# Ordering the transfers of a fused attention and FFN kernel by need, with part of its vector work and transposes moved to GpSimd and DMA

## Chip, cores, metric

One core of one Trainium2 chip. The metric is the device time of one execution in microseconds (us), lower is better.

## The reference, cut to what matters

Performer attention (random features, no softmax matrix) over 8 batches of 8 heads, 576 positions and head dimension 64, then a two-layer FFN with quick GELU over the 4608 tokens.

```python
def phi(x):                                   # x is q or k, scaled
    h = x @ omega.T - sum(x*x)/2              # 128 features
    return np.exp(h - h.max(-1)) / np.sqrt(m)
kv  = k_p^T @ v;  z = k_p.sum(positions)      # per head
num = q_p @ kv;   den = q_p @ z + 1e-6
x   = (num / den) as 4608 x 512
out = quick_gelu(x @ w_in) @ w_out            # 512 -> 2048 -> 512
```

## The kernel before

An attention **round** `p` handles two heads of one batch, four rounds to a batch. `item_pk` and `item_pq` project k and q and take the exponential, `vp` is v divided by the row maximum of k's features, `item_kv` and `item_nd` are the two products with it, and `item_xt` transposes the result `xb` into `xt`, the FFN's input. Other tiles named below: `kT` and `qT` are the transposed k and q, `sk` and `sq` their casts in DRAM, `kvs` is the copy of the `kv` product, `xps` TensorE's transpose of `xb` before it is copied, `gT` the FFN's hidden layer after the GELU, `win` and `wout` the FFN's weights, `osb` the output. The FFN works on nine **blocks** of 512 tokens; between its groups of four matmuls the rounds of a later batch are strewn. Only TensorE's order is fixed by hand; on the other engines a scheduler orders the instructions.

```python
def load_cast(b, n, h0, h1):      # f32 DRAM -> bf16 DRAM scratch, issued by GpSimd
    nc.gpsimd.dma_start(tiles[b]["s" + n][...], rows[...])
def load_tr(b, n, h0, h1):        # scratch -> transposed SBUF tile, issued by SyncE
    nc.sync.dma_start_transpose(tiles[b][n][...], tiles[b]["s" + n][...])
# ... cut: load_v, load_win, load_wout ...

def item_pk(p, i):
    pk = ps_pp.tile(...)          # six matmuls on 64 rows, 128 columns each
    nc.scalar.activation(out=ke, in_=pk, func=AF.Exp, scale=SCALE)
    nc.vector.reduce_max(out=maxE[:], in_=ke6, axis=AX.X)
    nc.vector.reciprocal(out=emax[:], in_=maxE[:])
    nc.vector.tensor_tensor(out=vp[:, :, 0:64], in0=v, in1=emax, op=ALU.mult)   # forms cut
    nc.vector.tensor_copy(out=vp[:, :, 64], in_=emax[:])

def item_xt(p):
    for t, c0 in enumerate(CHUNKS):
        nc.tensor.transpose(xps[:, c0 : c0 + 128], xb[:, t, :], ident[:])
    nc.vector.tensor_copy(out=xt[c][:, b * S : (b + 1) * S], in_=xps[:])

# a round: pk 0, kv, pk 1, nd 0, pq 0, nd 1, pq 1, xt  (the old round's items between the new one's)
ctx.enter_context(tc.manual_schedule(engines={mybir.EngineType.PE}))
# casts of batch 0, its v and transposes, all of win, batch 1, all of wout; then
for i in range(NBLK + 1):
    if i + 2 < B:
        load_batch(i + 2)
    # FFN groups of block i and i - 1, with the items of four rounds between them
```

The softmax here doesn't subtract the row's maximum and nothing guards it: scores larger than these inputs give would overflow.

Of the kernel before, what the change touches and what calls it, by code (L numbers as in the profile page):

```python
# [20 lines left out]
def kernel(  # L21
# [10 lines left out]
    nc = tc.nc  # L32
# [75 lines left out]
    def load_cast(b, n, h0, h1):  # L108
        rows = qrows if n == "q" else krows
        r0 = b * H * S2  # L110
        nc.gpsimd.dma_start(
            tiles[b]["s" + n][h0 * S2 : h1 * S2, :], rows[r0 + h0 * S2 : r0 + h1 * S2, :]
        )
# [20 lines left out]

    st = {}

    def item_pk(p, i):
        b, h = p // NPAIR, (p % NPAIR) * 2 + i
        kT = tiles[b]["k"]
        pk = ps_pp.tile([128, 2, 512], F32, name="pk", tag="pp")  # L140
        for c in range(3):
            for par in range(2):
                lo = par * 64
                nc.tensor.matmul(  # L144
                    pk[0:KP, par, c * 128 : (c + 1) * 128],
                    lhsT=kT[lo : lo + 64, h * S2 + c : (h + 1) * S2 : 3],
                    rhs=omT2[lo : lo + 64, :],
                )
        ke = work.tile([KP, 2, 384], BF16, name="ke", tag="ke")
        nc.scalar.activation(out=ke[:], in_=pk[0:KP, :, 0:384], func=AF.Exp, scale=SCALE)  # L150
        ke6 = ke[:].rearrange("p two (c f) -> p (two c) f", c=3)
        maxE = small.tile([KP, 6], F32, name="maxE", tag="maxE")
        nc.vector.reduce_max(out=maxE[:], in_=ke6, axis=AX.X)  # L153
        vp = work.tile([KP, 6, 65], BF16, name="vp", tag="vp")
        emax = small.tile([KP, 6], F32, name="emax", tag="emax")
        nc.vector.reciprocal(out=emax[:], in_=maxE[:])
        nc.vector.tensor_tensor(  # L157
            out=vp[:, :, 0:64].rearrange("p (two c) d -> p two c d", two=2),
            in0=tiles[b]["v"][:, h, :].rearrange("p (c two d) -> p two c d", c=3, two=2),
            in1=emax[:].rearrange("p (two c) -> p two c", two=2).unsqueeze(3).to_broadcast([KP, 2, 3, 64]),  # L160
            op=ALU.mult,
        )
        nc.vector.tensor_copy(out=vp[:, :, 64], in_=emax[:])
        st[p, "ke", i] = ke
        st[p, "vp", i] = vp

    def item_pq(p, i):
        b, h = p // NPAIR, (p % NPAIR) * 2 + i
        qT = tiles[b]["q"]
        pq = ps_pp.tile([128, 2, 512], F32, name="pq", tag="pp")  # L170
        for par in range(2):
            lo = par * 64
            nc.tensor.matmul(  # L173
                pq[:, par, 0:S2],
                lhsT=omT2[lo : lo + 64, :],
                rhs=qT[lo : lo + 64, h * S2 : (h + 1) * S2],
            )
        qe = work.tile([128, S], BF16, name="qe", tag="qe")
        nc.scalar.activation(  # L179
            out=qe[:].rearrange("p (two r) -> p two r", two=2),  # L180
            in_=pq[:, :, 0:S2],
            func=AF.Exp,
            scale=SCALE,
        )
        st[p, "qe", i] = qe

    def item_kv(p):
        kv = ps_m.tile([128, 2, 65], F32, name="kv", tag="m")
        for i in range(2):
            ke, vp = st.pop((p, "ke", i)), st.pop((p, "vp", i))  # L190
            for t in range(6):
                nc.tensor.matmul(  # L192
                    kv[:, i, :],
                    lhsT=ke[:, t // 3, (t % 3) * 128 : (t % 3 + 1) * 128],
                    rhs=vp[:, t, :],
                    start=(t == 0),
                    stop=(t == 5),
                )
        kvs = work.tile([128, 2, 65], BF16, name="kvs", tag="kvs")
        nc.scalar.activation(out=kvs[:], in_=kv[:], func=AF.Copy)  # L200
        st[p, "kvs"] = kvs

    def item_nd(p, i):
        if i == 0:
            st[p, "xb"] = work.tile([128, NCH, 128], BF16, name="xb", tag="xb")
        xb, kvs, qe = st[p, "xb"], st[p, "kvs"], st.pop((p, "qe", i))
        nd = ps_m.tile([128, NCH, 65], F32, name="nd", tag="m")
        for t, c0 in enumerate(CHUNKS):
            nc.tensor.matmul(nd[:, t, :], lhsT=qe[:, c0 : c0 + 128], rhs=kvs[:, i, :])  # L209
        rden = small.tile([128, NCH], F32, name="rden", tag="rden")  # L210
        nc.vector.reciprocal(out=rden[:], in_=nd[:, :, 64])  # L211
        nc.vector.tensor_tensor(  # L212
            out=xb[:, :, i * 64 : (i + 1) * 64],
            in0=nd[:, :, 0:64],
            in1=rden[:].unsqueeze(2).to_broadcast([128, NCH, 64]),
            op=ALU.mult,
        )

    def item_xt(p):
        b, c = p // NPAIR, p % NPAIR  # L220
        xb = st.pop((p, "xb"))
        st.pop((p, "kvs"))
        xps = ps_m.tile([128, S], BF16, name="xps", tag="m")
        for t, c0 in enumerate(CHUNKS):
            nc.tensor.transpose(xps[:, c0 : c0 + 128], xb[:, t, :], ident[:])  # L225
        nc.vector.tensor_copy(out=xt[c][:, b * S : (b + 1) * S], in_=xps[:])  # L226

    NP = B * NPAIR

    def round_items(p):  # L230
        its = []
        if p < NP:
            its.append(lambda: item_pk(p, 0))
        if p >= 1:
            its.append(lambda: item_kv(p - 1))
        if p < NP:
            its.append(lambda: item_pk(p, 1))
        if p >= 1:
            its.append(lambda: item_nd(p - 1, 0))
        if p < NP:  # L240
            its.append(lambda: item_pq(p, 0))
        if p >= 1:
            its.append(lambda: item_nd(p - 1, 1))
        if p < NP:
            its.append(lambda: item_pq(p, 1))
        if p >= 1:
            its.append(lambda: item_xt(p - 1))
        return its


    gTs = {}
# [22 lines left out]
    def mm2(i, r, part, pool, tag):  # L274
        if part == 0:
            pos[0] = pool.tile([128, DM], F32, name="po", tag=tag)
        po = pos[0]
        gT = gTs[i]
        for f in range(part * 4, part * 4 + 4):
            nc.tensor.matmul(  # L280
                po[:],
                lhsT=gT[:, f, r * 128 : (r + 1) * 128],
                rhs=wout[:, f, :],
                start=(f == 0),
                stop=(f == NFC - 1),
            )
        if part == 3:
            osb = osbp.tile([128, DM], F32, name="osb", tag="osb")
            nc.scalar.activation(out=osb[:], in_=po[:], func=AF.Copy, scale=0.5)  # L289
            c0 = i * TB + r * 128  # L290
            end = c0 + 128
            p0 = 0
            while c0 < end:
                run = c0 // S2
                n = min(end, (run + 1) * S2) - c0
                row = (run // 2) * S + 2 * (c0 - run * S2) + run % 2
                nc.sync.dma_start(
                    out[row : row + 2 * n - 1 : 2, :], osb[p0 : p0 + n, :]
                )
                c0 += n  # L300
                p0 += n


    ctx.enter_context(tc.manual_schedule(engines={mybir.EngineType.PE}))

    load_begin(0)
    for n in ("k", "q"):
        load_cast(0, n, 0, 2)
    for n in ("k", "q"):
        load_cast(0, n, 2, H)  # L310
    load_v(0, 0, 2)
    for n in ("k", "q"):
        load_tr(0, n, 0, 2)
    load_v(0, 2, H)
    for n in ("k", "q"):
        load_tr(0, n, 2, H)
    for j in range(4):
        load_win(j)
    load_batch(1)
    for j in range(4):  # L320
        load_wout(j)

    for p in range(NPAIR + 1):
        for it in round_items(p):
            it()

    for i in range(NBLK + 1):
        if 2 <= i + 2 < B + 0 and i + 2 < B:
            load_batch(i + 2)
        items = []  # L330
        for p in range((i + 1) * NPAIR + 1, (i + 2) * NPAIR + 1):
            if p <= NP:
                items += round_items(p)
        quanta = []
        for f in range(NFC):
            if i < NBLK:
                quanta.append((mm1, (i, f)))
            if i > 0:
                quanta.append((mm2, (i - 1, f // 4, f % 4, ps_o, "po")))
        done = 0  # L340
        for n, (fn, args) in enumerate(quanta):
            fn(*args)
            want = (n + 1) * len(items) // len(quanta)
            while done < want:
                items[done]()
                done += 1


# [28 lines left out]
```

## Time and profile before

| | us |
|---|---|
| time, median of 16 runs | 452.43 |
| span of the profiled execution | 450.0 |
| start-up, to the first `ph` matmul (first FFN layer) | 104.1 |
| block 0, to the first `po` matmul (second FFN layer) | 43.3 |
| blocks 1 to 6, with attention rounds between | 226.2 |
| blocks 7 and 8, FFN alone | 55.2 |
| last second layer, with its eviction `osb` | 17.3 |
| end, from the last `osb` | 3.9 |

Each stage is read off the timeline as the distance between two starts (the end: from the end of the last `osb`); the stages add up to the span. (The prediction put the border of block 7 at 374.4 by calculation; the timeline has the first `po` of block 7 at 373.58, which moves 0.9 us between two rows.)

### The profile page before, as it was taken

To read this page: it belongs to the slowest core of one execution; us is meant where nothing else is said; L and a number is where in the kernel's file an instruction comes from. 1 tells how busy PE (TensorE), PEld (TensorE's weight loads), DVE (VectorE), ACT (ScalarE), POOL (GpSimd) and SP (SyncE) were. 2 spreads that over 40 slices of the span, in tenths; PEclk is the share of its full clock that TensorE was granted. 3 is DMA by queue.
4 is the path that set the end of the run, shared out by engine and by line. 5 is a ranking of instruction groups with operands and counts; after the bars stand their busy time and mean duration, and the time that the engine had idled before them with its cause. 6 is when DMAs were issued, how large, how long until landed. Compare 5 with 4: busy or idle time off the path is not lost.

```text
span 450.0 us, 6365 instructions
## 1 busy us (share of the span) xinstructions
PE 344.3 (77%) x2529; PEld 164.6 (37%) x2529; DVE 253.0 (56%) x563; ACT 198.8 (44%) x341; POOL 15.8 (4%) x32
## 2 busy tenths in 40 slices
PE   0001000466677999999999999999999999999985
PEld 0000000243333444444444444444444444444432
DVE  0200300466766788877888877888776774334300
ACT  1110100354445556656665566655655654444311
POOL 6211100000000000000000000000000000000000
PEclk9999999999988999999999999999999999999999
DMA  9999999664046009215801901830010011010121
GB/s 213 221 210 196 222 214 214 146 134 78 1 90 122 19 30 200 59 25 131 151 25 42 217 25 42 178 87 25 23 47 26 23 25 47 25 47 31 41 59 59
DMA packets 54302, 42.39 MB, mean 94 GB/s; under 512 B 38912, under 2 KB 49152, under 8 KB 53760
## 3 DMA queue, kind: packets, MB, share of 16 engines
q1 hardware_dynamic: 49248, 28.35, 27.3%
q0 software_dynamic: 5024, 13.63, 15.3%
q8 instruction: 20, 0.33, 0.3%
q14 instruction: 10, 0.08, 0.1%
HBM read 36.73 MB, written 18.87 MB: 124 GB/s over the span
## 4 chain that ended last, share of the span: by engine, by line
PE 71%; DMA 17%; DVE 8%; ACT 2%; issue 1%; POOL 0%; POOLq 0%; ACTq 0%
PE po L280 30%; PE ph L259 27%; DMA qT<-sq 11%; DMA wout<-in_moe_w_out_dram 4%; PE pk L144 4%; PE kv L192 3%; PE pq L173 3%; PE xps L225 3%; DMA sq<-in_q_dram 2%; PE nd L209 2%; DVE maxE L153 2%; DVE gT L268 2%; DVE vp L157 2%; DVE xb L212 1%; ACT ke L150 1%
## 5 line engine op out<-in xcount | busy, mean ns | idle before, releaser
L259 PE MATMUL ph<-xt,win 128*128 128x512 bf16 x576 | 152.6, 387 | 0.2 <-DVE xt L226 0.2
L280 PE MATMUL po<-wout,gT 128*128 128x512 bf16 x576 | 146.7, 380 | 2.8 <-ACT osb L289 2.8
L268 DVE SCALAR_TENSOR_TENSOR gT<-th,ph 128x512 bf16<-128x512 bf16 x144 | 98.4, 684 | 81.7 <-ACT th L267 81.2
L267 ACT ACTIVATE th<-ph 128x512 bf16<-128x512 f32 x144 | 86.0, 597 | 126.9 <-PE ph L259 126.5
L153 DVE TENSOR_REDUCE maxE<-ke 96x6 f32<-96x768 bf16 x64 | 60.6, 949 | 44.7 <-ACT ke L150 44.5
L280 PEld LDWEIGHTS <-gT 128*128 128x128 bf16 x576 | 48.9, 98 | 58.3 <-issue 4.3
L150 ACT ACTIVATE ke<-pk 96x768 bf16<-96x768 f32 x64 | 51.0, 799 | 37.3 <-PE pk L144 36.3
L259 PEld LDWEIGHTS <-win 128*128 128x128 bf16 x576 | 50.4, 100 | 43.9 <-issue 2.9
L179 ACT ACTIVATE qe<-pq 128x576 bf16<-128x576 f32 x64 | 41.2, 645 | 53.3 <-PE pq L173 53.2
L173 PE MATMUL pq<-qT,omT 64*128 64x288 bf16 x128 | 20.4, 318 | 45.9 <-DMA qT<-sq 45.9
L144 PE MATMUL pk<-omT,kT 64*96 64x128 bf16 x384 | 27.9, 257 | 29.0 <-DMA kT<-sk 29.0
L144 PEld LDWEIGHTS <-kT 64*96 64x96 bf16 x384 | 18.4, 150 | 54.7 <-DMA kT<-sk 29.7
L209 PE MATMUL nd<-kvs,qe 128*128 128x65 bf16 x320 | 21.9, 203 | 18.4 <-DVE xb L212 18.4
L157 DVE TENSOR_TENSOR vp<-vst,emax 96x384 bf16<-96x384 f32 x64 | 35.3, 551 | 0.8
L173 PEld LDWEIGHTS <-omT 64*128 64x128 bf16 x128 | 6.3, 94 | 70.9 <-issue 59.8
L211 DVE RECIPROCAL rden<-nd 128x5 f32<-128x5 f32 x64 | 11.7, 183 | 35.9 <-PE nd L209 35.9
L212 DVE TENSOR_TENSOR xb<-nd,rden 128x320 bf16<-128x320 f32 x64 | 31.1, 486 | 1.1
L289 ACT ACTIVATE osb<-po 128x512 f32<-128x512 f32 x36 | 21.5, 597 | 20.3 <-PE po L280 19.1
L209 PEld LDWEIGHTS <-qe 128*128 128x128 bf16 x320 | 18.0, 102 | 33.0 <-DVE xb L212 21.1
L192 PEld LDWEIGHTS <-ke 96*128 96x128 bf16 x384 | 17.4, 103 | 6.7
L192 PE MATMUL kv<-vp,ke 96*128 96x65 bf16 x384 | 19.0, 201 | 0.2
L226 DVE COPY xt<-xps 128x576 bf16<-128x576 bf16 x32 | 14.6, 456 | 7.6 <-PE xps L225 7.6
(21 smaller groups left out, 78.2 us busy)
## 6 DMA issues: line engine op xcount, KB each, us to landing
vst<-in_v_dram SPq DMA_DIRECT2D x7, 1152.0 KB, 7.5
out_dram<-osb SPq DMA_DIRECT2D x24, 256.0 KB, 2.0
sk<-in_k_dram POOLq DMA_DIRECT2D x7, 576.0 KB, 23.7
sq<-in_q_dram POOLq DMA_DIRECT2D x7, 576.0 KB, 23.2
win<-in_moe_w_in_dram POOLq DMA_DIRECT2D x4, 512.0 KB, 18.5
wout<-in_moe_w_out_dram POOLq DMA_DIRECT2D x4, 512.0 KB, 27.0
out_dram<-osb SPq DMA_DIRECT2D x8, 192.0 KB, 2.3
out_dram<-osb SPq DMA_DIRECT2D x8, 128.0 KB, 2.4
```

What stands on the lines that cost most here:

```text
L144: nc.tensor.matmul(pk[0:KP, par, c * 128 : (c + 1) * 128], lhsT=kT[lo : lo + 64, h * S2 + c : (h + 1) * S2 : 3], rhs=omT2[lo : lo + 64, :],)
L150: nc.scalar.activation(out=ke[:], in_=pk[0:KP, :, 0:384], func=AF.Exp, scale=SCALE)
L153: nc.vector.reduce_max(out=maxE[:], in_=ke6, axis=AX.X)
L157: nc.vector.tensor_tensor(out=vp[:, :, 0:64].rearrange("p (two c) d -> p two c d", two=2), in0=tiles[b]["v"][:, h, :].rearrange("p (c two ...
L173: nc.tensor.matmul(pq[:, par, 0:S2], lhsT=omT2[lo : lo + 64, :], rhs=qT[lo : lo + 64, h * S2 : (h + 1) * S2],)
L179: nc.scalar.activation(out=qe[:].rearrange("p (two r) -> p two r", two=2), in_=pq[:, :, 0:S2], func=AF.Exp, scale=SCALE,)
L192: nc.tensor.matmul(kv[:, i, :], lhsT=ke[:, t // 3, (t % 3) * 128 : (t % 3 + 1) * 128], rhs=vp[:, t, :], start=(t == 0), stop=(t == 5),)
L209: nc.tensor.matmul(nd[:, t, :], lhsT=qe[:, c0 : c0 + 128], rhs=kvs[:, i, :])
L259: nc.tensor.matmul(ph[:], lhsT=win[:, c, f * 128 : (f + 1) * 128], rhs=xt[c][:, i * TB : (i + 1) * TB], start=(c == 0), stop=(c == CM - 1),)
L267: nc.scalar.activation(out=th[:], in_=ph[:], func=AF.Tanh, scale=0.851)
L268: nc.vector.scalar_tensor_tensor(out=gT[:, f, :], in0=th[:], scalar=1.0, in1=ph[:], op0=ALU.add, op1=ALU.mult)
L280: nc.tensor.matmul(po[:], lhsT=gT[:, f, r * 128 : (r + 1) * 128], rhs=wout[:, f, :], start=(f == 0), stop=(f == NFC - 1),)
```

## The change

The intent: bring the data in the order in which it is needed, relieve VectorE and TensorE of work that others can do, and space the items of a round so that no hand-off is waited for. GpSimd's and SyncE's order is now fixed by hand too. The diff, cut:

```diff
-def item_pk(p, i): ...        # and item_pq(p, i)
+def item_qk(p, i):            # pk's six matmuls, pq's two, then both exponentials
-        nc.vector.tensor_tensor(out=vp[:, :, 0:64], ...)
+        eng = nc.gpsimd if p <= 2 * NPAIR else nc.vector
+        eng.tensor_tensor(out=vp[:, :, 0:64], ...)
-        nc.vector.tensor_copy(out=vp[:, :, 64], in_=emax[:])
+        eng.tensor_copy(out=vp[:, :, 64], in_=emax[:])
 def item_xt(p):
+        if c == NPAIR - 1 or b == 1:     # TensorE and a copy, as before
+        else:
+            nc.sync.dma_start_transpose(dst[:, 0:512], xb[:, 0:4, :])      # forms cut
+            nc.sync.dma_start_transpose(dst[:, 512:S], xb[64:128, 4, :])
-# a round: pk 0, kv, pk 1, nd 0, pq 0, nd 1, pq 1, xt
+# a round: qk 0, kv, (empty), nd 0, qk 1, nd 1, (empty), xt
-                nc.sync.dma_start(out[...], osb[...])
+                nc.gpsimd.dma_start(out[...], osb[...])
-    manual_schedule(engines={PE})
+    manual_schedule(engines={PE, Pool, SP})
+    # batch 0's casts and transposes in three parts, v of two heads first
+    startup = {
+        0: [batch1],                                       # after round 0
+        3: [lambda: loads("i0", "i1")],                    # half of win
+        4: [lambda: loads("i2", "i3"), lambda: casts(2), lambda: loads("o0", "o1")],
+    }
 for i in range(NBLK + 1):
-        load_batch(i + 2)
+        load_v(i + 2, 0, H); load_tr(i + 2, "k", 0, H); load_tr(i + 2, "q", 0, H)
+        # in the middle of block i > 0: casts(i + 3);  after block 0: loads("o2", "o3"), casts(3)
```

More of the change, by code (lines that the diff above doesn't have):

```diff
@@ L135 @@
     st = {}
-    def item_pk(p, i):
+    def item_qk(p, i):
         b, h = p // NPAIR, (p % NPAIR) * 2 + i
-        kT = tiles[b]["k"]
+        kT, qT = tiles[b]["k"], tiles[b]["q"]
         pk = ps_pp.tile([128, 2, 512], F32, name="pk", tag="pp")
+        pq = ps_pp.tile([128, 2, 512], F32, name="pq", tag="pp")
         for c in range(3):
-            for par in range(2):
-                lo = par * 64
+            for lo in (0, 64):
                 nc.tensor.matmul(
-                    pk[0:KP, par, c * 128 : (c + 1) * 128],
+                    pk[0:KP, lo // 64, c * 128 : (c + 1) * 128],
                     lhsT=kT[lo : lo + 64, h * S2 + c : (h + 1) * S2 : 3],
@@ L148, in item_pk @@
                 )
-        ke = work.tile([KP, 2, 384], BF16, name="ke", tag="ke")
-        nc.scalar.activation(out=ke[:], in_=pk[0:KP, :, 0:384], func=AF.Exp, scale=SCALE)
-        ke6 = ke[:].rearrange("p two (c f) -> p (two c) f", c=3)
-        maxE = small.tile([KP, 6], F32, name="maxE", tag="maxE")
-        nc.vector.reduce_max(out=maxE[:], in_=ke6, axis=AX.X)
-        vp = work.tile([KP, 6, 65], BF16, name="vp", tag="vp")
-        emax = small.tile([KP, 6], F32, name="emax", tag="emax")
-        nc.vector.reciprocal(out=emax[:], in_=maxE[:])
-        nc.vector.tensor_tensor(
-            out=vp[:, :, 0:64].rearrange("p (two c) d -> p two c d", two=2),
-            in0=tiles[b]["v"][:, h, :].rearrange("p (c two d) -> p two c d", c=3, two=2),
-            in1=emax[:].rearrange("p (two c) -> p two c", two=2).unsqueeze(3).to_broadcast([KP, 2, 3, 64]),
-            op=ALU.mult,
-        )
-        nc.vector.tensor_copy(out=vp[:, :, 64], in_=emax[:])
-        st[p, "ke", i] = ke
-        st[p, "vp", i] = vp
-    def item_pq(p, i):
-        b, h = p // NPAIR, (p % NPAIR) * 2 + i
-        qT = tiles[b]["q"]
-        pq = ps_pp.tile([128, 2, 512], F32, name="pq", tag="pp")
-        for par in range(2):
-            lo = par * 64
+        for lo in (0, 64):
             nc.tensor.matmul(
-                pq[:, par, 0:S2],
+                pq[:, lo // 64, 0:S2],
                 lhsT=omT2[lo : lo + 64, :],
@@ L177, in item_pq @@
             )
+        ke = work.tile([KP, 2, 384], BF16, name="ke", tag="ke")
+        nc.scalar.activation(out=ke[:], in_=pk[0:KP, :, 0:384], func=AF.Exp, scale=SCALE)
         qe = work.tile([128, S], BF16, name="qe", tag="qe")
@@ L184, in item_pq @@
         )
+        ke6 = ke[:].rearrange("p two (c f) -> p (two c) f", c=3)
+        maxE = small.tile([KP, 6], F32, name="maxE", tag="maxE")
+        nc.vector.reduce_max(out=maxE[:], in_=ke6, axis=AX.X)
+        vp = work.tile([KP, 6, 65], BF16, name="vp", tag="vp")
+        emax = small.tile([KP, 6], F32, name="emax", tag="emax")
+        nc.vector.reciprocal(out=emax[:], in_=maxE[:])
+        eng = nc.gpsimd if p <= 2 * NPAIR else nc.vector
+        eng.tensor_tensor(
+            out=vp[:, :, 0:64].rearrange("p (two c) d -> p two c d", two=2),
+            in0=tiles[b]["v"][:, h, :].rearrange("p (c two d) -> p two c d", c=3, two=2),
+            in1=emax[:].rearrange("p (two c) -> p two c", two=2).unsqueeze(3).to_broadcast([KP, 2, 3, 64]),
+            op=ALU.mult,
+        )
+        eng.tensor_copy(out=vp[:, :, 64], in_=emax[:])
+        st[p, "ke", i] = ke
+        st[p, "vp", i] = vp
         st[p, "qe", i] = qe
@@ L222, in item_xt @@
         st.pop((p, "kvs"))
-        xps = ps_m.tile([128, S], BF16, name="xps", tag="m")
-        for t, c0 in enumerate(CHUNKS):
-            nc.tensor.transpose(xps[:, c0 : c0 + 128], xb[:, t, :], ident[:])
-        nc.vector.tensor_copy(out=xt[c][:, b * S : (b + 1) * S], in_=xps[:])
+        if c == NPAIR - 1 or b == 1:
+            xps = ps_m.tile([128, S], BF16, name="xps", tag="m")
+            for t, c0 in enumerate(CHUNKS):
+                nc.tensor.transpose(xps[:, c0 : c0 + 128], xb[:, t, :], ident[:])
+            nc.vector.tensor_copy(out=xt[c][:, b * S : (b + 1) * S], in_=xps[:])
+            return
+        dst = xt[c][:, b * S : (b + 1) * S]
+        nc.sync.dma_start_transpose(
+            dst[:, 0:512].rearrange("p (t r) -> p t r", t=4),
+            xb[:, 0:4, :].rearrange("p t c -> p (t c)"),
+        )
+        nc.sync.dma_start_transpose(dst[:, 512:S], xb[64:128, 4, :])
     NP = B * NPAIR
     def round_items(p):
-        its = []
-        if p < NP:
-            its.append(lambda: item_pk(p, 0))
-        if p >= 1:
-            its.append(lambda: item_kv(p - 1))
-        if p < NP:
-            its.append(lambda: item_pk(p, 1))
-        if p >= 1:
-            its.append(lambda: item_nd(p - 1, 0))
-        if p < NP:
-            its.append(lambda: item_pq(p, 0))
-        if p >= 1:
-            its.append(lambda: item_nd(p - 1, 1))
-        if p < NP:
-            its.append(lambda: item_pq(p, 1))
-        if p >= 1:
-            its.append(lambda: item_xt(p - 1))
-        return its
+        new, old = p < NP, p >= 1
+        its = [
+            (new, lambda: item_qk(p, 0)),
+            (old, lambda: item_kv(p - 1)),
+            (old, None),
+            (old, lambda: item_nd(p - 1, 0)),
+            (new, lambda: item_qk(p, 1)),
+            (old, lambda: item_nd(p - 1, 1)),
+            (old, None),
+            (old, lambda: item_xt(p - 1)),
+        ]
+        return [fn for on, fn in its if on]
     gTs = {}
@@ L296, in mm2 @@
                 row = (run // 2) * S + 2 * (c0 - run * S2) + run % 2
-                nc.sync.dma_start(
+                nc.gpsimd.dma_start(
                     out[row : row + 2 * n - 1 : 2, :], osb[p0 : p0 + n, :]
@@ L301, in mm2, with casts, loads, batch1 @@
                 p0 += n
-    ctx.enter_context(tc.manual_schedule(engines={mybir.EngineType.PE}))
+    ET = mybir.EngineType
+    ctx.enter_context(tc.manual_schedule(engines={ET.PE, ET.Pool, ET.SP}))
     load_begin(0)
-    for n in ("k", "q"):
-        load_cast(0, n, 0, 2)
-    for n in ("k", "q"):
-        load_cast(0, n, 2, H)
+    load_begin(1)
     load_v(0, 0, 2)
-    for n in ("k", "q"):
-        load_tr(0, n, 0, 2)
-    load_v(0, 2, H)
-    for n in ("k", "q"):
-        load_tr(0, n, 2, H)
-    for j in range(4):
-        load_win(j)
-    load_batch(1)
-    for j in range(4):
-        load_wout(j)
+    for h0, h1 in ((0, 2), (2, 4), (4, H)):
+        for n in ("k", "q"):
+            load_cast(0, n, h0, h1)
+    for h0, h1 in ((0, 2), (2, 4), (4, H)):
+        for n in ("k", "q"):
+            load_tr(0, n, h0, h1)
+        if h0 == 0:
+            load_v(0, 2, H)
+    def casts(b):
+        load_begin(b)
+        load_cast(b, "k", 0, H)
+        load_cast(b, "q", 0, H)
+    def loads(*names):
+        for n in names:
+            {"i": load_win, "o": load_wout}[n[0]](int(n[1]))
+    def batch1():
+        load_cast(1, "k", 0, H)
+        load_cast(1, "q", 0, H)
+        load_tr(1, "k", 0, H)
+        load_tr(1, "q", 0, H)
+        load_v(1, 0, H)
+    startup = {
[3 more added lines that the diff above has]
+    }
     for p in range(NPAIR + 1):
-        for it in round_items(p):
+        for it in filter(None, round_items(p)):
             it()
+        for fn in startup.get(p, []):
+            fn()
     for i in range(NBLK + 1):
-        if 2 <= i + 2 < B + 0 and i + 2 < B:
-            load_batch(i + 2)
+        if i + 2 < B:
+            load_v(i + 2, 0, H)
+            for n in ("k", "q"):
+                load_tr(i + 2, n, 0, H)
         items = []
@@ L344 @@
             while done < want:
-                items[done]()
+                if items[done]:
+                    items[done]()
                 done += 1
+            if 0 < i and n == 16 and i + 3 < B:
+                casts(i + 3)
+        if i == 0:
+            loads("o2", "o3")
+            casts(3)
 _INS = ['q', 'k', 'v', 'omega', 'moe_w_in', 'moe_w_out']
```

## The prediction

> **What bounds the kernel now.** I read the page's slices first, then the waits by stage, then the queue views, then the timeline for the stage borders. The slices (40 of 11.25 us) show three stages.
>
> ```profile
> PE   0001000466677999999999999999999999999985
> DMA  9999999664046009215801901830010011010121
> GB/s 213 221 210 196 222 214 214 146 134 78 1 90 122 19 30 200 59 25 131 151 25 42 217 25 42 178 87 25 23 47 26 23 25 47 25 47 31 41 59 59
> ```
>
> For seven slices (79 us) TensorE does nothing and the DMA engines are full; then it is 40 to 70% busy up to slice 13 (146 us); then it is at 90% or more to the end. The waits of TensorE, asked for the window 0 to 85 us (first two lines) and 85 to 150 us (third), say on what; from 150 to 330 us there are none.
>
> ```profile
> PE pq L173 <- DMA qT<-sq: 45.9, 2, 35.7
> PE pk L144 <- DMA kT<-sk: 29.0, 2, 15.5
> ...
> PE nd L209 <- DVE xb L212: 17.9, 7, 2.9
> ```
>
> So batch 0's transposed k and q are late. Two source-line views say why: L111 are the casts of k and q into DRAM scratch (issued by GpSimd), L116 the transposes that read it (issued by SyncE).
>
> ```profile
> L111 POOL DMA_DIRECT2D sk<-in_k_dram x9: 488/493/625, 1.2 to 56.3; - x9
> L111 POOL DMA_DIRECT2D sq<-in_q_dram x9: 488/493/527, 2.2 to 59.1; - x9
> ...
> L116 SPq DMA_TRANSPOSE qT<-sq x9: 2145/4620/19368, 8.9 to 289.1; - x9
> DMA to landing us min/median/max: 4.1/6.7/48.4
> ```
>
> All nine casts of each tensor, that is all eight batches, start within the first 59 us, though batch 7 is wanted after 300 us. With them go all weights. A transpose that lands in 4.1 us alone took 48.4 us. Sum of the slices: the first seven moved 1490 x 11.25 us = 16.8 MB.
>
> The stage borders are from the timeline and the chain of waits (start, length, work):
>
> ```profile
> 104.10 1.91 PE L259 MATMUL ph<-xt,win 128*128 128x512 bf16 x4
> ...
> 147.40 1.04 PE L280 MATMUL po<-wout,gT 128*128 128x512 bf16 x4
> ...
> 155.27 0.44 PE L225 MATMUL xps<-ident,xb 128*128 128x128 bf16 x5
> 155.55 1.03 PE L259 MATMUL ph<-xt,win 128*128 128x512 bf16 x4
> 156.51 0.42 PE L144 MATMUL pk<-omT,kT 64*96 64x128 bf16 x6
> ...
> 165.97 0.41 PE L144 MATMUL pk<-omT,kT 64*96 64x128 bf16 x6
> ...
> 428.81 3.63 PE po L280 x16
> ```
>
> The first FFN matmul is at 104.1, the first second-layer one at 147.4. So: start-up 104.1 us; block 0 with attention rounds 43.3 us; then rounds of 9.46 us (156.51 to 165.97), four to a block, six blocks, 227 us; two blocks without attention, up to 428.8, 54.3 us; the last second layer 17.3 us to 446.1; output and end 3.9 us. Sum 450.0, the span; the time is 1.8 us more.
>
> **What the Trainium skill says.** (1) "DMA: Bandwidth & Descriptors", section "Issuing engines are not separate DMA queues": transfers from all issuers end on the same 16 engines and interleave. The trace agrees: SyncE's 48.4 us transpose ran beside GpSimd's casts at full DMA share. (2) "GPSIMD Engine Reference", section "3.1 Elementwise — side-by-side cycle accounting": a two-input elementwise operation needs about 2.6 cycles per element. At the 1.2 GHz of its specification, 384 elements are an estimate of 0.83 us, about 1.0 with dispatch. No run shows it yet; VectorE's same operation (L157) takes 0.551. (3) "TensorE: Matmul & The Clock Gate", section "Why this matters for your kernels": idle gaps of over about 3 us send the clock back to half. The trace agrees roughly: after waits of 2.9 us in block 0, groups of four ph matmuls took 1.90 us against 1.03. (4) "VectorE: DVE Perf Modes", section "The three transpose paths": a 128x128 bf16 transpose by DMA is 1309 ns. Four and a half of them one after another are an estimate of 5.9 us for each xt; no run shows it yet.
>
> **The change part by part.**
>
> Start-up (the large part). Casts are issued in program order, two batches ahead, and weights after round 3. Each batch is 1.18 MB as cast, 1.18 MB of v and 1.18 MB transposed (from the sizes in the DMA issues), 3.54 MB. Before the first FFN matmul the kernel now needs two batches and a quarter of win: 2 x 3.54 + 0.52 = 7.6 MB; at the 213 GB/s of the first seven slices 36 us. The dependent chain gives a second figure. Rounds in the old start-up take 6.73 us each (timeline: nd at 88.86, 95.59, 102.32). New round, from row means: rden 0.2, maxE 0.95, xb 0.49, emax 0.18, vp on GpSimd 1.3 (estimate with the small copy), kv 0.82, kvs 0.28, nd 0.46, rden 0.2, xb 0.49, nd 0.46 = 5.83, with hand-offs 6.1 us. First operands at about 10 us (old: 16.6, under contention), first kv about 15.5, then three rounds to the fourth kv at 33.8, nd and the last xt to about 38. Batch 1's casts wait on GpSimd behind the first vp pair (about 15 us), so its transposes land near 33, just in time; win comes after round 3's vp, near 34, and lands about 41. I take 41 us for the first FFN matmul: 63 us less.
>
> Block 0. vp leaves VectorE: per round 2 x (0.551 + 0.171) = 1.4 us. VectorE then has per round 4 x 0.684 + 2 x (0.949 + 0.184 + 0.183 + 0.486) + 0.456 = 6.8 us, TensorE 16 x 0.216 + 2.9 = 6.3 us. Empty slots put more work between the two nd, which is where the 2.9 us waits stood (that row is 17.9 us in all, about 12 of it here). The order of VectorE's instructions puts maxE of the second head behind the second nd, but kv now has some 3.6 us of TensorE work ahead of it against 3.1 of chain. I take 7.6 us a round, 30.5 us for the block: 13 us less.
>
> Six full blocks. TensorE is the only bound, and 3 of 4 xps groups go: in start-to-start they cost 0.28 us (155.27 to 155.55), not the 0.44 busy. 18 x 0.28 = 5 us less. pk and pq next to each other cost TensorE the same; ACT gets two exps in one burst of 1.45 us, with over 3 us between an FFN group and the next use of its buffer. Thus 222 us.
>
> Block 1: wout's second half is only issued after the last vp of block 0, and wanted about 6.5 us into block 1. I add 1.5 us of stall.
>
> Last blocks 54.3 and 17.3 us, as before. Output goes through GpSimd: I add 0.9 us to the 3.9, as nothing hides the last one.
>
> Sum: 41 + 30.5 + 222 + 1.5 + 54.3 + 17.3 + 4.8 = 371.4; with 1.8 us, 373. As most of what I may have missed is waits, I put it at 376.
>
> **The rivals.**
>
> Rival 1, a new in-order wait takes back part of the start-up. GpSimd's queue now mixes vp, casts and weights, SyncE's the batch transposes and the xt ones; each blocks what stands behind it. For it: the fence above shows a SyncE issue up to 19.4 us long under load, and win is issued late. Against it: there is half the traffic. If win or batch 1 comes 15 us late, the time is 391.
>
> Rival 2, VectorE or the round chain stays the bound of block 0, because GpSimd's vp is slower than VectorE's and lies on the chain. For it: 0.55 us becomes about 1. Against it: off VectorE's queue, it no longer delays xb. Block 0 then stays at 38 to 43 us: 384 to 388.
>
> Rival 3, the time saved at the start is paid back later, since casts move into the full blocks and xt by DMA is added there. For it: a batch's casts took about 5.6 us of full DMA (the bursts after 60 us). Against it: those blocks show a DMA share of about 0.41, casts add some 0.15 and xt 0.1; loads are asked for a block ahead. If it bites at 2 us a block, 388.
>
> Rival 4, the gain was mostly hidden anyway. TensorE's idle 80 us lies at the head of the chain with nothing beside it, so I give this almost nothing.
>
> **Range and chances.** Start-up between 35 and 50, block 0 between 28 and 39, the steady blocks 0 to 6 us worse, wout 0 to 5: taken together about -12 and +19 around 376. So 364 to 395. Even with rivals 1 to 3 together it stays under 430, so faster by over 2% is nearly sure.
>
> **What would show it.** Right: first ph matmul near 41 us and first po near 72; no casts of batches 3 to 7 before that; waits of pk and pq on DMA well under 25 us; rounds of 9.2 us in the full blocks; L225 on TensorE about 55 matmuls. Wrong: ph waiting for win or xt, po for wout by over 5 us, kv waiting for vp by over 1 us a round in block 0, rounds over 9.5 us later, or a single vp on GpSimd of 2 us or more.

## The result, and the profile after

The changed kernel took 378.74 us (median of 11 runs, 377.38 to 380.65). The ratio to the kernel before is 0.8364, 95% interval 0.8339 to 0.8388. Ratios are the mean time of one kernel's fast runs over that of the other's of the same rounds, so they are not quite the ratio of the medians quoted.

| stage | before | predicted | after |
|---|---|---|---|
| start-up | 104.1 | 41 | 43.9 |
| block 0 | 43.3 | 30.5 | 38.4 |
| blocks 1 to 8 | 281.4 | 222 + 1.5 + 54.3 = 277.8 | 269.6 |
| last second layer | 17.3 | 17.3 | 17.2 |
| end | 3.9 | 4.8 | 7.9 |
| span | 450.0 | 371.4 | 377.1 |

The borders, from the timeline after (start, length in us, work, idle time before in brackets): first `ph`, first `po`, two successive rounds of a full block, and the first `po` of block 7.

```profile
43.89 1.89 PE L256 MATMUL ph<-xt,win 128*128 128x512 bf16 x4 [0.79 <-DMA win<-in_moe_w_in_dram]
...
82.31 1.04 PE L277 MATMUL po<-wout,gT 128*128 128x512 bf16 x4
...
119.54 0.41 PE L144 MATMUL pk<-omT,kT 64*96 64x128 bf16 x6
...
128.29 0.41 PE L144 MATMUL pk<-omT,kT 64*96 64x128 bf16 x6
...
296.69 1.02 PE L277 MATMUL po<-wout,gT 128*128 128x512 bf16 x4
```

The slices (now 9.43 us each) have lost their empty head. The DMA engines are still full for eight slices, 75 us, but TensorE works beside them.

```profile
PE   0337688498999999999999999999999999999880
DMA  8999999939999639936791878121122011001110
```

The casts, from the view of their source line, are now spread over the run, and land in 7.6 us at the median where it was 22.4:

```profile
L111 POOL DMA_DIRECT2D sk<-in_k_dram x10: 488/525/642, 1.3 to 209.6; - x10
...
DMA to landing us min/median/max: 3.5/7.6/15.9
```

TensorE's waits, from the windows 0 to 50 us (first two lines) and 50 to 85 us:

```profile
PE pk L144 <- DMA kT<-sk: 11.4, 2, 8.7
PE pq L150 <- DMA qT<-sq: 5.4, 1, 5.4
...
PE xps L221 <- DVE xb L207: 4.3, 4, 1.2
PE pk L144 <- DMA kT<-sk: 2.6, 1, 2.6
PE pq L150 <- DMA qT<-sq: 1.5, 1, 1.5
```

Of 75 us of waits for transposed q and k, 21 are left, 17 of them in the start-up. The last two lines are new in kind: in the last round of block 0, TensorE waits for batch 2. The `nd` waits on `xb` of block 0 (11.5 us between 104 and 147 us of the kernel before) are gone; a smaller one of `xps` on `xb` stands in their place.

Two rows from the page's groups answer what `vp` costs on the two engines:

```profile
L171 DVE TENSOR_TENSOR vp<-vst,emax 96x384 bf16<-96x384 f32 x46 | 25.4, 552 | 0.9
L171 POOL TENSOR_TENSOR vp<-vst,emax 96x384 bf16<-96x384 f32 x18 | 14.9, 830 | 52.8 <-DVE emax L169 44.5
```

So the range held, but three terms were off by about 8 us or less and partly cancelled: block 0 was 7.9 us longer than forecast, blocks 1 to 8 8.2 us shorter, the end 3.1 us longer. The experiments had two aims: to show what made the start-up short, and to find the causes of these three.

### The profile page after: what moved, and what is told of

It reads as the page before. It is cut to its first block, busy times and chain, and to the rows that moved or that the text cites. A ratio compares the mean times of both kernels' runs of the same rounds, so it can differ in the third digit from the quotient of the medians.

```text
span 377.1 us, 6257 instructions
## 1 busy us (share of the span) xinstructions
PE 326.7 (87%) x2424; PEld 158.2 (42%) x2424; DVE 233.4 (62%) x506; ACT 196.6 (52%) x341; POOL 60.6 (16%) x118
## 4 chain that ended last, share of the span: by engine, by line
PE 70%; DMA 9%; DVE 8%; ACT 3%; issue 3%; SPq 3%; POOL 2%; POOLq 0%
PE ph L256 30%; PE po L277 29%; DMA qT<-sq 5%; PE pk L144 4%; PE kv L187 3%; PE nd L204 2%; DVE gT L265 2%; DVE maxE L166 2%; DMA wout<-in_moe_w_out_dram 2%; SPq L116 2%; ACT th L264 2%; PE pq L150 2%; DMA win<-in_moe_w_in_dram 1%; DMA sq<-in_q_dram 1%; DVE xb L207 1%
## 5 line engine op out<-in xcount | busy, mean ns | idle before, releaser
L277 PEld LDWEIGHTS <-gT 128*128 128x128 bf16 x576 | 52.3, 98 | 69.5 <-issue 14.2
L294 POOL DMA_DIRECT2D out_dram<-osb x48 | 26.0, 544 | 255.7 <-ACT osb L286 255.7
L204 PEld LDWEIGHTS <-qe 128*128 128x128 bf16 x320 | 18.8, 102 | 18.4 <-issue 4.5
L171 DVE TENSOR_TENSOR vp<-vst,emax 96x384 bf16<-96x384 f32 x46 | 25.4, 552 | 0.9
L171 POOL TENSOR_TENSOR vp<-vst,emax 96x384 bf16<-96x384 f32 x18 | 14.9, 830 | 52.8 <-DVE emax L169 44.5
```

The lines of the kernel that those rows point to most:

```text
L171: eng.tensor_tensor(out=vp[:, :, 0:64].rearrange("p (two c) d -> p two c d", two=2), in0=tiles[b]["v"][:, h, :].rearrange("p (c two d) -> ...
L204: nc.tensor.matmul(nd[:, t, :], lhsT=qe[:, c0 : c0 + 128], rhs=kvs[:, i, :])
L277: nc.tensor.matmul(po[:], lhsT=gT[:, f, r * 128 : (r + 1) * 128], rhs=wout[:, f, :], start=(f == 0), stop=(f == NFC - 1),)
```

## The experiments

All twelve gave correct results. Each was timed beside the kernel before; experiments are set against the changed kernel by these ratios (0.8364; run again as the tenth experiment, 0.8381).

### 1 and 2: what keeps the transfers in order

Nothing in the data makes a cast of batch 2 wait, and GpSimd issues what stands next in its queue. The theory is that `vp` on GpSimd, whatever it saves VectorE, holds the transfers behind it.

```diff
 # e1_vp_dve
-        eng = nc.gpsimd if p <= 2 * NPAIR else nc.vector
+        eng = nc.vector
 # e2_vp_dve_paced: the same, and
-        eng.tensor_copy(out=vp[:, :, 64], in_=emax[:])
+        (nc.gpsimd if p <= 2 * NPAIR else nc.vector).tensor_copy(out=vp[:, :, 64], in_=emax[:])
```

> Both vp operations back on VectorE, nothing else changed. Theory (the vp operations on GpSimd pace its DMA queue: casts and weights behind them cannot be issued before the attention round in front of them has run): with nothing to wait for, GpSimd issues batch 1's to 3's casts and all weights within the first 20 us, batch 1's transposes come late again, the first ph matmul moves from 43.9 us to between 60 and 80, total 393 to 412. Rival (vp's place matters only as VectorE load, the DMA order alone is enough): first ph within 5 us of 43.9, total 378 to 386.

> vp's large multiplication on VectorE in all rounds, but its 6-element copy stays on GpSimd up to round 8, so that GpSimd's queue waits as before. Theory (pacing is what matters): first ph within 3 us of 43.9, no burst of casts, total 376 to 384, block 0 up to 4 us longer since VectorE has 8 x 0.55 us more in it. Rival (VectorE's load matters): block 0 from 38.4 to over 43, total over 386.

Measured: e1 401.38 us (ratio 0.887, 0.8852 to 0.8889), first `ph` at 72.8; e2 377.23 us (ratio 0.8339, 0.8324 to 0.8355), first `ph` at 43.3 and first `po` at 81.8. Between the two only the place of a 6-element copy differs, and it is worth 24 us. The timeline of GpSimd shows how. First e1, where `win`, batch 2's casts and `wout` follow one another from 5.7 us on:

```profile
5.67 0.78 POOL L84 DMA_DIRECT2D win<-in_moe_w_in_dram  x1
...
10.43 0.53 POOL L111 DMA_DIRECT2D sk<-in_k_dram  x1 [0.66 <-DMA sk<-in_k_dram]
...
14.67 0.78 POOL L90 DMA_DIRECT2D wout<-in_moe_w_out_dram  x1 [2.29 <-DMA sk<-in_k_dram]
```

Then e2, where the copy of round 3 stands in front of `win`:

```profile
36.31 0.21 POOL L177 CAST vp<-emax 96x6 bf16<-96x6 f32 x1 [2.62 <-DVE emax L169]
36.80 1.54 POOL L84 DMA_DIRECT2D win<-in_moe_w_in_dram  x2 [0.28 <-issue]
```

Without the pacing, TensorE's waits for transposed k and q up to 80 us are 47.6 us, with it 19.7. Moving `vp`'s multiplication off VectorE is worth nothing measurable in the total: e2's interval overlaps that of the changed kernel. In an undisturbed round of block 0 it is worth 0.3 us (`pk` at 52.75 and 60.40, 7.65 us, against 7.35), but there the last round waits for batch 2 in both. The rival, that the order of the lists is enough, is refuted by e1: with everything but the pacing the first `ph` went from 104.1 to 72.8 us, and the pacing brought it from there to 43. (The last casts of e1, batch 3's, went out at 32.5 us, not within the 20 that I expected.)

### 3: split pk and pq again

```diff
-    qk 0, kv, (empty), nd 0, qk 1, nd 1, (empty), xt
+    pk 0, kv, pq 0, nd 0, pk 1, nd 1, pq 1, xt
```

> pk and pq in separate slots again (in the order of the kernel before), all else as changed. Theory (each change from 64-row to 128-row matmuls costs 0.11 us and a lone pq pair 0.11 more, so that joining them saved 0.22 us a head): rounds of full blocks 8.75 to about 9.2 us, total +9 to +13, 387 to 392. Rival (rounds are shorter only because VectorE and ACT wait less): rounds stay at 8.7 to 8.85, total 377 to 381.

Measured: 383.75 us, ratio 0.8482 (0.8449 to 0.8515), about 5 us over the changed kernel. A round of the full blocks took 9.18 us (`pk` at 117.23 and 126.41), as the theory said; from the first `po` to the last `osb` the kernel took 294.6 us against 286.3, 8.3 more. The total rose less than I expected, because start-up and block 0 were 3.5 us shorter (first `ph` 42.6, first `po` 78.8). Batch 2's q came at 72.9 us in both, but with `pq` in a slot of its own, `kv` and a group of `ph` ran before that wait and not behind it; the wait was 1.2 us against 4.1 in all, and the `ph` group behind it took 1.03 us against 1.90. The chains of both, in time order (start, length, work), first the changed kernel:

```profile
119.61 0.34 PE pk L144 x6
119.96 0.12 PE pq L150 x2
120.08 0.97 PE po L277 x4
...
122.30 0.86 PE po L277 x4
```

then e3:

```profile
117.31 0.34 PE pk L144 x6
117.65 0.97 PE po L283 x4
...
119.87 0.23 PE pq L174 x2
120.10 0.97 PE po L283 x4
```

A group of four `po` takes 0.97 us behind a 64-row group and 0.86 otherwise, and a `pq` pair 0.23 alone and 0.12 behind `pk`. Joining saves 0.22 us a head, 0.44 a round; measured 9.18 - 8.75 = 0.43. In every fourth round it was only 0.21 (9.64 - 9.43); I did not look into why.

### 4: xt on TensorE throughout

```diff
-        if c == NPAIR - 1 or b == 1:
+        if True:
```

> All xt transposes on TensorE with VectorE's copy, no DMA transposes of xt. Theory (TensorE bounds the full blocks): 18 more groups of 0.28 us, rounds 8.75 to 8.96, total +4 to +7, 382 to 386. Rival (DMA traffic of xt costs as much as it saves): within 2 us of 378.7 or faster.

Measured: 385.2 us, ratio 0.8508 (0.8456 to 0.8559): 6 us slower, so the DMA transposes pay. Rounds with an `xps` group took 9.03 us (`pk` at 120.40 and 129.43) against 8.75, the 0.28 of the prediction. In the start-up `xps` waited 7.0 us for `xb`, and the first `ph` moved to 48.2; block 0 became 33.1 us, with only 1.1 us of waits for batch 2: the later start left it time to come.

### 5: the last output from SyncE

```diff
-                nc.gpsimd.dma_start(
+                (nc.sync if i == NBLK - 1 else nc.gpsimd).dma_start(
```

> Only the output transfers of the last token block go from SyncE instead of GpSimd. Theory (the 6.9 us drain of GpSimd's queue after its last transfer stands alone at the end): the time from the last osb copy to the end falls from 7.9 to about 4 us, total 373.5 to 376. Rival (the end is the landing of the last output): within 1 us of 378.7.

Measured: 374.48 us, ratio 0.8229 (0.8172 to 0.8286). From the end of the last `osb` (370.0) to the end of the span (373.2) are 3.2 us, against 7.9. The lines are of the view of the source line that closes the program (count, minimum, median and maximum duration in ns, first and last start): before,

```profile
L372 POOLq DRAIN  x3: 40/93/23173, 59.0 to 449.7; - x3
```

after,

```profile
L395 POOLq DRAIN  x3: 46/93/6854, 369.4 to 376.8; - x3
```

GpSimd's queue ends with a drain of its own transfers. Before, it had issued its last at 59.1 us, and the 23 us of drain lay beside the attention rounds. After, it starts behind the last output at 369.4 and takes 6.9 us, of which the transfer, landing at the median in 2.4 us, accounts for the first third; what the rest is, no run shows. In e5 the drain still took 6.5 us, but began at 353.4, beside the last matmuls.

### 6: wout later

```diff
-        4: [lambda: loads("i2", "i3"), lambda: casts(2), lambda: loads("o0", "o1")],
+        4: [lambda: casts(2), lambda: loads("i2", "i3")],
+            if i == 0 and n == 8:  loads("o0", "o1")      # in block 0
+            if i == 0 and n == 12: loads("o2", "o3")
```

> Batch 2's casts ahead of the second half of win, and wout's two halves moved into block 0 (after its second and third round). Theory (block 0's last round waits for batch 2's transposes because wout and win share the full DMA engines with them): waits of pk and pq on DMA in block 0 from 4.1 us to under 1, first po from 82.3 to 75 to 79, total 372 to 376. Rival (the DMA engines have too much in all, the order doesn't matter): the wait moves to po on wout, total within 2 us of 378.7.

Measured: 373.48 us, ratio 0.8251 (0.822 to 0.8282). The waits of `pk` and `pq` on DMA between 50 and 90 us are gone from TensorE's list, and block 0 took 32.1 us (43.9 to 76.0). The list in that window now:

```profile
PE xps L221 <- DVE xb L207: 4.7, 4, 1.2
PE po L277 <- DMA wout<-in_moe_w_out_dram: 1.1, 2, 0.7
PE nd L204 <- ACT kvs L195: 0.8, 3, 0.3
```

So what block 0 had too much was the collision of batch 2's transfers with `wout` and the second half of `win` (the edit moves both, so their shares are not told apart), and the order does matter: batch 2's casts had landed, and the transposes that read them started, at 51.3 us, where the changed kernel had 58.8. The lost time, 6.3 us, was more than the 4.1 us of waits: after such a wait, groups of four `ph` took 1.90 us where they take 1.03 elsewhere in the block, and the granted clock between 60 and 80 us was 0.83 (1.00 in e6). The changed kernel's timeline there:

```profile
70.99 0.41 PE L144 MATMUL pk<-omT,kT 64*96 64x128 bf16 x6 [2.61 <-DMA kT<-sk]
...
73.86 1.90 PE L256 MATMUL ph<-xt,win 128*128 128x512 bf16 x4
```

### 7: the order of the transfers alone

The kernel before, with the new start-up lists, casts two batches ahead, output on GpSimd, and only `vp`'s small copy on GpSimd to pace it. Items, transposes and multiplications are as before.

> The kernel before with only the order of transfers changed: the new start-up lists, casts two batches ahead, output and vp's small copy on GpSimd as its pacing; item order, pk and pq apart, xt by TensorE and vp's multiplication on VectorE as in the kernel before. Theory (transfer order gives about 60 of the 74 us): first ph at 44 to 50, block 0 40 to 44 us, rounds 9.46, end 8 us after the last output copy, total 393 to 403. Rival (the reordered rounds are what shortens the start-up): first ph later than 55, total over 406.

Measured: 396.46 us, ratio 0.8777 (0.8745 to 0.881). Stages: start-up 44.8, block 0 42.1, blocks 1 to 6 226.2 as before, end 7.9. Block 0 still has the old waits of `nd`:

```profile
PE nd L209 <- DVE xb L212: 10.9, 4, 2.7
```

So the order of the transfers, with its pacing, gives 56 of the 74 us. The other 18 are 3.7 in block 0, 11.8 in blocks 1 to 6, and little else. The 3.7 is what was left after the collision that e6 removes: against e6's 32.1 us, the new rounds are worth 10 us in block 0.

### 8 to 10: the two mended terms together, and one step more

e8 is 5 and 6 together. e9 also splits batch 0's `v`, heads 4 to 7 behind the transposes. The tenth is the changed kernel again, on the same chip.

```diff
 # e9_v_split
-        if h0 == 0: load_v(0, 2, H)
+        if h0 == 0: load_v(0, 2, 4)
+    load_v(0, 4, H)
```

> The two mended terms together: wout late as in e6_wout_late and the last block's output from SyncE as in e5_last_out_sp. Theory (the two costs lie in different stages and add): first po near 76, 3.2 to 4 us from the last osb copy to the end, total 368 to 371. Rival (the end only hides another wait): within 1 us of e6_wout_late's 373.5.

> e8_both with v of batch 0's heads 4 to 7 loaded after batch 0's transposes and not before them. Theory (the transfers of the start-up share full DMA engines, so what goes ahead of q and k delays them): the 4.6 us wait of pq on qT falls under 3, first ph 1 to 3 us earlier than 43.9, total 366 to 370. Rival (the start-up is bound by the sum of all transfers up to win, not by their order): first ph within 1 us of 43.9, total as e8_both.

> The changed kernel unaltered, for comparison on the same chip: 377.5 to 380.5 us, ratio to the kernel before 0.836.

Measured: e8 368.02 us (ratio 0.815, 0.8125 to 0.8174); e9 376.07 us (0.8321, 0.8291 to 0.8351); the changed kernel 379.41 us (0.8381). e8 is 11 us or 3% below the changed kernel, the sum of both gains within the noise.

e9's total fits neither of its theories. What was expected of it took the 4.6 us wait of `pq` on `qT` and the 43.9 of the first `ph` from e6; its base e8 had 2.0 us and 41.6 in its own profile, so e9's 1.7 us and 43.0 show no gain from the split. The time was lost in waits of `ph` (timeline of TensorE):

```profile
43.01 0.61 PE L256 MATMUL ph<-xt,win 128*128 128x512 bf16 x1 [3.84 <-DMA win<-in_moe_w_in_dram]
...
53.78 1.01 PE L256 MATMUL ph<-xt,win 128*128 128x512 bf16 x2 [8.84 <-DMA xt<-xb]
```

The `xt` transposes, issued by 39.3 us, landed up to 15.8 us later. GpSimd had issued batch 2's casts at 41.3 us, in among them. But so it had in e8, at 40.1 us, with only 2.2 us of `ph` waiting for `xt`; why the same neighbours cost 8.8 us in e9's order is not shown.

### 11 and 12: is it batch 2's casts?

Both put batch 2's casts behind the first `vp` of block 0 in GpSimd's queue, so that they cannot start before the first `ph` has its `xt`; e11 on e8, e12 on e9.

```diff
-        4: [lambda: casts(2), lambda: loads("i2", "i3")],
+        4: [lambda: loads("i2", "i3")],
+            if i == 0 and n == 0:     # then also v and the transposes of batch 2
+                casts(2)
```

> e8_both with batch 2's casts behind the first vp of block 0 on GpSimd, so that they can't start before the first ph. Theory (xt's transposes, issued by 38 us, land late because batch 2's casts come among them): the 2.2 us wait of ph on xt goes, first ph 40 to 41.6, no new wait on batch 2's transposes, total 366 to 369. Rival (casts are then too late): pk or pq wait over 2 us on DMA at the end of block 0, total over 370.

> The same edit on e9_v_split. Theory (e9_v_split lost its time only in the 8.8 us wait of ph on xt behind batch 2's casts): that wait falls under 3 us, first ph at 41 to 43, first po 75 to 79, total 366 to 370. Rival (xt's transposes land late whatever stands behind them, for example because batch 1's and 2's v loads stand beside them): the wait stays over 5 us, total over 373.

Measured: e11 368.19 us (ratio 0.8133, 0.8107 to 0.8159), the same as e8; e12 369.72 us (0.8158, 0.8135 to 0.8182). In e12 the longest wait of `ph` on `xt` fell from 8.8 to 2.5 us, and 6 us came back: batch 2's casts were the cause of that wait. The `xt` transposes of the start-up still took up to 9.8 us to land, so they are not the only one. The sum of the waits on `xt` was 3.1 us, just over the 3 I had set, the first `ph` came at 43.8, not 41 to 43, and the first `po` at 80.4, not 75 to 79. In e11 the wait on `xt` was gone, but the first `ph` stood at 44.6 against the 40 to 41.6 that I expected: `pq` waited 6.0 us for `qT` in that run, where e8 had 2.0. The edit does not touch that wait: the changed kernel, e5, e6 and e10 have the same code up to it and show 5.4, 5.7, 4.6 and 6.1 us, so e8's 2.0 was the exception. The first `ph`, too, differs between two profiles of the same start-up: 43.9 in the changed kernel and 45.3 in e10, 43.9 in e6 and 41.6 in e8. Differences of 1 to 2 us in it between two experiments show nothing. No order that I tried brought the first `ph` below 41.6 us; in the start-up the DMA engines are full throughout, and a transfer moved forward puts another back. That the sum of the transfers is the limit there is my inference from this and from the 36 us of the prediction; no run cut the bytes.

## Why the prediction was right, point by point

- **Start-up, right.** Forecast 41 us, measured 43.9. e7 gives 44.8 with no change but the order of transfers and its pacing, so the cause is the one named. `win` was issued at 38.2 us and landed in 5.7, where the forecast had it issued near 34 and landed at 41. What the prediction had only half seen is what keeps the order: it listed "each blocks what stands behind it" as the danger of rival 1, and e1 shows that this blocking is what earns about 29 us of the start-up (72.8 against 43.9).
- **Block 0, round right, size of the block wrong (38.4 for 30.5).** The undisturbed rounds were as forecast: `pk` at 53.62 and 60.97, 7.35 us for 7.6, where the old order of items takes 10.2 (e7, `pk` at 65.86 and 76.08). But "vp leaves VectorE", 1.4 us of VectorE's work a round, brought only 0.3 (e2), and joining `pk` and `pq` brought nothing here (7.12 us in e3, `pk` at 55.69 and 62.81). That leaves the order of the items, with more work between the two `nd`; this is by elimination, as no run changed it alone. The missing term is rival 1 in a place where I had not put it: batch 2's casts and transposes, beside `win` and `wout` in full DMA engines. e6 removes that collision and leaves 32.1 us. The working had costed only VectorE and TensorE in this stage.
- **Full blocks, the step was wrong (8.75 us a round for about 9.2).** "pk and pq next to each other cost TensorE the same" was the failed sentence. e3 shows 0.43 us a round for it; the 0.28 us of each `xps` group was right (e4).
- **wout, right in size**: the forecast was 1.5 us of stall, and `po` waited 1.8 us in all.
- **vp on GpSimd, somewhat cheaper than estimated**: 0.830 + 0.208 us against 1.3 for both. Rival 2 gave a wrong weight to it: where it runs makes no measurable difference to the total (e2).
- **The end, mis-sized.** 0.9 us was added for an output through GpSimd and 4.0 measured; the term is the drain of its queue (e5).
- **Rival 3, no.** The DMA share between 100 and 180 us rose to about 0.8, more than the 0.66 of the working (0.41 + 0.15 + 0.1), and no round was longer than before but the first of block 1 (10.77 us against 9.45), the one that waits for `wout`.
- **The clock, read loosely.** Not every wait of 2.9 us was followed by slow matmuls: behind the `nd` wait of 2.84 us a group of four `ph` took 1.03 us, behind those of 2.87 to 2.89 it took 1.90 (kernel before, block 0).

The sum was right to within 1% with errors (measured less forecast) of +2.9 in the start-up, +7.9, -8.2 and +3.1 us, and about 3 us added for waits not foreseen; so part of the accuracy of 376 for 379 is luck. The start-up, 63 of the 76 us forecast, is not.

## What to carry to other kernels

Here a DMA queue without anything to wait for ran far ahead (the casts of all eight batches within 59 us), and the early transfers were paid for by those that were needed first. When the DMA engines are full, look at what each transfer is for, and let the queue wait on the computation: an instruction that depends on it, in the same in-order queue, is enough, even a tiny one (24 us in e2 against e1). Then watch what the pacing releases when a stage gets faster, put matmuls of equal row count next to each other (0.43 us a round in e3), and let the queue whose end must be drained finish early (4.7 us at the end in e5).

## What the Trainium skill lacked or had wrong

- "DMA: Bandwidth & Descriptors", section "Rules for kernel authors", advises to issue a DMA early and wait late, to overlap it with compute. It sets no bound to "early": here the casts of all eight batches within 59 us held back the first batch, and ordering and pacing the transfers gave 56 of 452 us (e7). Its semaphore waits are for a DMA that depends on another; that page does not show how to hold back one that depends on nothing (e1 and e2: 24 us for the place of a 6-element copy).
- "TensorEngine Tiling (Array Packing)", section "Key Properties", says that a change of tiling mode drains TensorE, without a cost. Here a group of four 128-row matmuls took 0.97 us behind 64-row ones and 0.86 otherwise, and joining two 64-row groups saved 0.43 us a round (e3). That the drain is the cause was not tested apart from this.
- No page gives the cost of the drain that follows GpSimd's last transfer (a small constant is given for the drains at a program's beginning and end, which does not cover it): 6.5 to 6.9 us here, hidden in e5, where the last transfer was issued earlier.
- "GPSIMD Engine Reference", section "3.1 Elementwise — side-by-side cycle accounting": the 2.6 cycles per element fit well, 0.830 us measured for an estimate of 0.83. The page's ratio of about 2 to VectorE, which is for 2048 elements of fp32, was 830 / 552 = 1.5 here, for 384 elements with a bf16 result.
- "VectorE: DVE Perf Modes", section "The three transpose paths": the 1309 ns of one DMA transpose must not be added up, as the prediction did. Four blocks in one transfer landed in 2.5 us at the median, not the 5.2 that this estimate gives; under load it took up to 9.5 us in this kernel and 15.8 in e9.
